# Attention and mixture of experts on one core: conditional weight copies for the first expert tiles, a shorter square root, W2's maxima on ScalarE, and a new order

## The chip, the core and the metric

The kernel runs on one core of one Trainium2 chip, as one program. Its time is device microseconds (us) of one execution. The engines of the core are TensorE (PE, with its weight loads as PEld), VectorE (DVE), ScalarE (ACT), GpSimd (POOL) and SyncE (SP, which here only issues DMA transfers).

## What is computed

An attention with pooled keys feeds a mixture of experts; every row goes to the one expert with the highest logit.

```python
# attention: B, N, C = 4, 12288, 128
kv_pool = kv.reshape(B, 96, 4, 8, 4, C).mean(axis=(2, 4))
k = v = kv_pool.reshape(B, 768, C) @ w_sr
s = (q @ k.transpose(0, 2, 1)) / sqrt(C)
a = exp(s - s.max(-1)); a /= a.sum(-1) + 1e-9
x = (a @ v).reshape(49152, C)
# experts: E, F = 8, 1024
xn = x / (norm(x) + 1e-6); en = emb / (norm(emb) + 1e-6)
logits = xn @ en.T / tau
expert = argmax(logits); gate = softmax(logits)[expert]
for e in range(E):
    out[expert == e] = gate * (relu(x[expert == e] @ w1[e]) @ w2[e])
```

## The kernel before

**Steps, groups and tiles.** The 49152 rows are 96 steps of 512 rows (24 per batch). A step loads its q (`q_load`), transposes it, multiplies it with k in four quarters (`s_mm`, 128 rows by 768 keys each), takes the maximum of each quarter (`s_max`, DVE), the exponential (`s_exp`, ACT), splits the result into a high and a low half (`p_hi` on ACT or DVE, `p_lo` on DVE or POOL), turns both by transposing DMAs (`p_t`) and multiplies them with v (`av`), then normalizes (`x_norm`, `x_mul`). In the first `kf` steps ("unscaled") s is computed in f32 from one copy of k instead of from f16 halves; the pairs of quarters marked in `em` ("unsplit") are transposed on PE (`p_turn`) and multiplied in f32, with no transposing DMA.

Four steps are a group: `group_ops` computes norms, logits, gates and the rank of every row within its expert and scatters the 2048 rows into `xs_rows`, a buffer sorted by expert (POOL, `g_scatter`). Per group, `select` then chooses the next 8 expert tiles (256 rows of one expert each) and writes for each its expert (`et`), its first row (`off_i`) and the row of its weights (`wi_i`); it runs on DVE for the first `sd` groups and on POOL for the rest, as a chain of small operations. The chain for the first 8 tiles (n = 0) starts when group 1 is ranked.

An expert tile loads its rows (`load`, L1551 and L1552) and its weights (`load_w`, L1541) into one of three weight buffers of 1026 KB, multiplies with W1 (`l1`), splits into `hh` (ACT, L1582) and `hl` (DVE, L1587), multiplies with W2 (`l2`), scales (`o_out`) and scatters into the output. For tiles marked A in `om` the gate is first multiplied with the scale that lies behind the weights (`o_gate`, L1622, DVE), and ACT writes the output; for the others DVE does it in one operation.

**Conditional copies.** The SP instruction of `load_w` copies only if `w < E * P`. `weight_rows` adds 4096 to the row when the tile has the same expert as the tile three before, whose weights are still in that buffer. It does so from tile 8 on; the first 8 tiles have no comparison and always copy.

**Weights.** `w_ops` loads W1 and W2 of each expert in the first 180 us, takes their maxima on DVE (`w_max`, L1187), makes a power of two from them (`pow2`), splits both into f16 halves and stores them to `w_prep`.

**Key and value pooling.** For batches 1 to 3, `kv_load` fetches each batch's keys in 8 pieces of 768 KB (L449), and DVE adds up each piece with four operations (`kv_adds`, L463).

**The order.** Each engine runs its instructions in the order in which they were written. That order comes from a planner (`Plan.run`): each piece of work has an engine, a duration, a key (its due time) and its dependencies, and the planner writes the ready piece with the lowest key. Transfers are modelled by `moved`, one running sum of the durations given as `dma`. The keys come from the numbers in `X`: `da` and `di` (length of a step), `kv` and `kvs` (how many steps ahead pieces of keys are loaded, and how far apart), `kv1` and `kvs1` (the same for batch 1), `lead` (how far ahead a tile's rows are loaded), and the strings of letters that choose an engine for each repetition of an operation. 16 steps (`ka`) run before the first expert tile; from there to step 96 each step is mixed with two expert tiles.

## Time and profile before

| | |
|---|---|
| runs of the kernel | 1978.6, 1984.32, 1983.66 us; median 1983.66 us |
| the profiled execution | 1983.56 us; its span from the first to the last instruction is 1981.9 us |
| TensorE's granted clock, mean | 0.992 of full speed |
| PE busy | 1921.1 us (97%) |
| PEld busy | 1687.6 us (85%) |
| DVE busy | 1695.6 us (86%) |
| ACT busy | 1531.0 us (77%) |
| POOL busy | 1254.1 us (63%) |
| DMA | 335.86 MB, mean 169 GB/s |

Busy times are unions of the instructions of an engine; shares are of the span. A matmul that runs while the granted clock is low counts as busy for longer. A mean duration times a count can be above the busy time, since neighbours overlap by some tens of ns.

### The profile page before, as it was taken

How to read it: one execution, taken by the hardware profiler on the slowest of the kernel's cores; microseconds unless marked ns; L12 is line 12 of the kernel's file. 1: busy time of each engine (PE TensorE's matmuls, PEld its weight loads, DVE VectorE, ACT ScalarE, POOL GpSimd, SP SyncE). 2: the span in 40 equal slices, each digit the busy share in tenths (PEclk: the TensorE clock that was granted, in tenths of full speed). 3: DMA queues.
4: the chain of work that ended last, by engine and by line, in shares of the span. 5: the costliest groups of instructions: out<-in, count | busy, mean ns of one | idle time of the engine just before them, and what ended most of it. 6: DMA issues, size and time to landing. Idle time of an engine off the chain costs nothing. (4 is left out here: it accounts for less than half of the span.)

```text
span 1981.9 us, 63458 instructions
## 1 busy us (share of the span) xinstructions
PE 1921.1 (97%) x23400; PEld 1687.6 (85%) x23400; DVE 1695.6 (86%) x3870; ACT 1531.0 (77%) x3343; POOL 1254.1 (63%) x1828
## 2 busy tenths in 40 slices
PE   6999889999999999999999989999999999999997
PEld 4777678888888888888888878888888888899997
DVE  7799979999899988989999979988988888886654
ACT  3876867888888878888888868888888888775443
POOL 1547566685676676675875756756756766666653
PEclk9999999999999999999999999999999999999999
DMA  8996999998899998888988998788878878762261
GB/s 278 225 245 177 216 225 197 182 184 154 170 182 171 186 207 172 165 164 163 173 177 171 175 210 172 165 149 164 175 155 166 154 159 149 141 135 75 67 132 51
DMA packets 880475, 335.86 MB, mean 169 GB/s; under 512 B 828050, under 2 KB 839451, under 8 KB 877856
## 3 DMA queue, kind: packets, MB, share of 16 engines
q1 hardware_dynamic: 853088, 276.99, 71.7%
q0 software_dynamic: 24704, 53.53, 9.9%
q8 instruction: 185, 3.03, 0.6%
q10 hardware_dynamic: 2368, 1.25, 0.2%
q14 instruction: 130, 1.06, 0.2%
HBM read 263.01 MB, written 64.50 MB: 165 GB/s over the span
## 5 line engine op out<-in xcount | busy, mean ns | idle before, releaser
L1575 PE MATMUL ph<-x,wbuf 128*128 128x256 f16 x4536 | 615.8, 273 | 18.5 <-DVE hl L1587 14.1
L1582 ACT ACTIVATE hh<-ph 128x512 f16<-128x512 f32 x756 | 451.4, 598 | 190.6 <-PE ph L1575 151.7
L205 POOL DMA_INDIRECT out_dram<-o,m x388 | 417.3, 1075 | 280.0 <-ACT o L1631 63.6
L1587 DVE SCALAR_TENSOR_TENSOR hl<-ph,hh 128x512 f16<-128x512 f32 x756 | 515.4, 683 | 91.0 <-ACT hh L1582 85.3
L205 POOL DMA_INDIRECT xs_rows<-rows,pi x384 | 438.4, 1142 | 200.7 <-issue 32.6
L1575 PEld LDWEIGHTS <-wbuf 128*128 128x128 f16 x4656 | 432.9, 98 | 81.2 <-issue 18.0
L1611 PE MATMUL po<-wbuf,hh 128*128 128x128 f16 x6048 | 461.5, 220 | 1.5 <-DVE hl L1587 1.3
L1611 PEld LDWEIGHTS <-hh 128*128 128x128 f16 x6208 | 405.1, 98 | 29.6 <-issue 2.9
L815 DVE TENSOR_REDUCE nm<-s 128x1 f32<-128x768 f32 x384 | 364.1, 949 | 45.4 <-PE s L806 33.0
L806 PE MATMUL s<-k,qT 128*128 128x512 f16 (+1 forms) x1920 | 365.5, 327 | 2.9 <-ACT qT L768 1.3
L844 ACT ACTIVATE p<-s,nm,qa 128x768 f32<-128x768 f32 x320 | 317.5, 992 | 33.1 <-DVE nm L834 26.9
L931 PE MATMUL xp<-v,pthi 128*128 128x136 f16 x4416 | 323.6, 223 | 2.1 <-DVE t_cnt L1311 0.8
L885 DVE TENSOR_TENSOR plo<-p,phi 128x768 f16<-128x768 f32 x320 | 307.1, 961 | 2.3 <-ACT phi L868 1.8
L1611 PE MATMUL po<-wbuf,hl 128*128 128x128 f16 x3024 | 292.8, 220 | 0.1
L931 PEld LDWEIGHTS <-pthi 128*128 128x128 f16 x4416 | 281.8, 97 | 7.7 <-issue 2.7
L806 PEld LDWEIGHTS <-qT 128*128 128x128 f16 x1920 | 179.9, 98 | 90.3 <-issue 2.5
L868 ACT CAST phi<-p 128x768 f16<-128x768 f32 x289 | 240.8, 837 | 10.9 <-DMA pthi<-phi 7.2
L1611 PEld LDWEIGHTS <-hl 128*128 128x128 f16 x3104 | 206.3, 98 | 1.0 <-DVE hl L1587 0.3
L931 PE MATMUL xp<-v,ptlo 128*128 128x136 f16 x2208 | 193.0, 223 | 2.7 <-DMA ptlo<-plo 2.7
L951 ACT ACTIVATE x<-xp,rn 128x135 f32<-128x135 f32 x304 | 97.0, 373 | 80.0 <-DVE rn L943 64.4
L931 PEld LDWEIGHTS <-ptlo 128*128 128x128 f16 x2208 | 147.5, 98 | 3.0 <-DMA ptlo<-plo 2.9
L965 POOL TENSOR_TENSOR rows<-x,rows 128x256 f16<-128x256 f32 x192 | 133.5, 701 | 18.5 <-ACT rows L961 14.6
(402 smaller groups left out, 2050.2 us busy)
## 6 DMA issues: line engine op xcount, KB each, us to landing
wbuf<-w_prep SPq DMA_DIRECT2D x194, 1026.0 KB
q<-in_q_dram SPq DMA_DIRECT2D x96, 256.0 KB
kvt<-in_kv_dram SPq DMA_DIRECT2D x24, 768.0 KB
wf<-in_moe_w_dram SPq DMA_DIRECT2D x16, 512.0 KB
out_dram<-o,m POOLq DMA_INDIRECT x388
kvt<-in_kv_dram SPq DMA_DIRECT2D x12, 512.0 KB
xs_rows<-rows,pi POOLq DMA_INDIRECT x384
w_prep<-wo SPq DMA_DIRECT2D x8, 514.0 KB
```

Source lines behind the costliest of these rows:

```text
L205: ins = nc.gpsimd.indirect_dma_start(out=dst[:, :], out_offset=bass.IndirectOffsetOnAxis(ap=idx, axis=0), in_=src, in_offset=None, bounds_ ...
L806: nc.tensor.matmul(t[:, lo:hi], qs[:, l, :], r[:, lo:hi], start=i == 0, stop=i == 2)
L815: V.tensor_reduce(out=nm, in_=ks[k]["s", j], axis=AX.X, op=ALU.max, negate=True)
L844: nc.scalar.activation(out=p, in_=ks[k].pop(("s", j)), func=AF.Exp, bias=ks[k].pop(("nm", j)), scale=1.0 if unscaled(k) else ks[k]["fac"],)
L868: nc.scalar.copy(out=hi, in_=p)
L885: eng.tensor_tensor(out=lo, in0=ks[k].pop(("p", j)), in1=hi, op=ALU.subtract)
L931: nc.tensor.matmul(ks[k]["xp", h][:, i, :e], l[:, c, :], r[:, c, :e], start=n == 0, stop=n == len(terms) - 1, skip_group_check=True,)
L965: nc.gpsimd.tensor_tensor(out=r[:, :, C : 2 * C], in0=ks[k]["x"][:, 2 * h : 2 * h + 2, 0:C], in1=r[:, :, 0:C], op=ALU.subtract)
L1575: nc.tensor.matmul(ph[:, kk * n : (kk + 1) * n], wt[:, o + f : o + f + P], r, start=i == 0, stop=i == 2)
L1582: nc.scalar.activation(out=hh, in_=ts[t]["ph", u], func=AF.Relu)
L1587: V.scalar_tensor_tensor(out=hl, in0=ts[t].pop(("ph", u)), scalar=0.0, in1=ts[t]["hh", u], op0=ALU.max, op1=ALU.subtract)
L1611: nc.tensor.matmul(ts[t]["po"][:, j * C : (j + 1) * C], h[:, kk * n + j * P : kk * n + (j + 1) * P], wt[:, f : f + P], start=u == 0 and i ...
```

## The change

1. `select` for the first 8 tiles also compares experts. `weight_rows` now builds the comparison for t0 = 0 too; `fresh` sets it to 0 for tiles 0 to 2, which have no tile three before.
2. `rsqrt` with three rounds of three operations becomes `root`: a guess of the square root, a reciprocal, a product, a sum, and again a reciprocal, a product and a weighted sum. The `norm` product behind it goes. That is 8 DVE operations instead of 12 for each of 24 groups, and once for the expert embeddings.
3. For every expert (`wq` is all A) the maximum of |W2| on DVE is replaced by a sum of squares on ACT (`w_sq`, 128x1024 with accumulation) and two small DVE operations (`w_norm`) that make a power of two from its root. Its junk output goes to the buffer `wo0`, which is so taken earlier.
4. The fill of the rows past all experts (`dummies`, 1152 KB, ACT's queue) moves from 30 us to step 88.
5. The planner's numbers are new: `kf` 14 instead of 16, 10 unsplit pairs instead of 8, `sd` 0 (the first `select` on POOL too), other letters for the engines, and other costs of transfers (`late` adds 8 us after a piece of keys, weights of the first three tiles cost 3.6).

```diff
 X = dict(
-    ka=16, da=8.163, di=15.077, db=14.187, dma=1.729, ahead=2.284, av=10.802, av0=0.255, lb=-2.941, l2=2.467,
-    qt=1.558, lead=18.764, x=-17.373, r=-0.479, s=-1.235, p=14.303, x0=5.348, r0=2.658, s0=1.425, p0=5.773, qt0=0.912,
+    ka=16, da=5.621, di=18.693, db=14.346, dma=1.729, ahead=2.284, av=10.385, av0=-0.933, lb=-2.362, l2=2.65,
+    qt=1.523, lead=26.836, x=-82.128, r=-0.415, s=-1.976, p=13.972, x0=2.656, r0=5.014, s0=1.344, p0=7.404, qt0=0.282,
...
-    h=13.626, kv=20.599, kvs=2.297, w0=-12.3, start=17.487, early=21.36, wd=13.046, xw=1.718, qd=23, qs=16.452,
+    h=19.587, kv=27.46, kvs=2.934, w0=-19.499, start=8.415, early=21.36, wd=11.49, xw=1.718, qd=24, qs=17.772,
...
-    kf=16, kc="AD", kk=4.522, su=-1.263, vk=-3.85, om="DDAAADAD", og=2.102,
+    kf=14, kc="DA", kk=0.062, su=1.242, vk=-1.844, om="DDDAADDD", og=1.947,
 )
...
-                        ready = self.moved + X["dma"]
+                        ready = self.moved + X["dma"] + op.late
...
-        def square():
-            V.tensor_tensor(out=h["z"], in0=y(), in1=y(), op=ALU.mult)
-        def times():
-            V.scalar_tensor_tensor(out=h["z"], in0=h["z"], scalar=-0.5, in1=x(), op0=ALU.mult, op1=ALU.mult)
-        def update():
-            V.scalar_tensor_tensor(out=y(), in0=h["z"], scalar=1.5, in1=y(), op0=ALU.add, op1=ALU.mult)
-        return [halve, guess] + [square, times, update] * 3
+        def under():
+            V.reciprocal(out=h["z"], in_=y())
+        def over():
+            V.tensor_tensor(out=h["z"], in0=h["z"], in1=x(), op=ALU.mult)
+        def twice():
+            V.tensor_tensor(out=y(), in0=y(), in1=h["z"], op=ALU.add)
+        def mean():
+            V.scalar_tensor_tensor(out=y(), in0=y(), scalar=0.25, in1=h["z"], op0=ALU.mult, op1=ALU.add)
+        return [halve, guess, under, over, twice, under, over, mean]
...
+    def w_sq(e):
+        w_out(e, 0)
+        nc.scalar.activation(out=ws[e]["wo", 0][:, 0:F], in_=ws[e]["w", 1], func=AF.Square, accum_out=ws[e]["m"][:, 1:2])
...
+        def fresh():
+            V.memset(h["same"][:, 0:WB], 0.0)
...
-        return [weights, same, skip, cast] if t0 >= WB else [weights, cast]
+        return [weights, same, *([] if t0 else [fresh]), skip, cast]
...
-    x_dummies = add("ACT", 0.1, 30.0, dummies, dma=3.1, hold=True)
+    x_dummies = add("ACT", 0.1, slot(NSTEP - 8, 0), dummies, dma=3.1, hold=True)
...
-            o = took("kvt", add("SP", 0.45, t0, lambda h=h: kv_load(b, h), *turn("kvt", 2), dma=2.6, hold=True))
+            o = took("kvt", add("SP", 0.45, t0, lambda h=h: kv_load(b, h), *turn("kvt", 2), dma=2.7, hold=True, late=8.0))
...
-                m.append(add("DVE", 1.14, v + 0.9 * d, lambda e=e, i=i: w_max(e, i), o, *deps))
...
+                if i and X["wq"][e] == "A":
+                    o = took("wo0", add("ACT", 1.2, v + 0.9 * d, lambda e=e: w_sq(e), o, *deps, *turn("wo0", 1)))
+                    m.append(add("DVE", 0.36, v + 0.9 * d, lambda e=e: w_norm(e), o))
```

What this moves is shown at three places. In the rows, a name ends in a number that grows in the order in which the planner wrote the program, so a piece of work with a higher number was written later; `hl_3_25893` is the low half of the fourth block of a tile's hidden units.

The first place is SP's queue at the second change of experts (tiles 96 to 98), where three copies of weights are made in a row and pieces of batch 3's keys are loaded. Before:

```order
L1541 DMA wbuf_2844<-w_prep 128x4104
L449 DMA kvt_6_25625<-in_kv_dram 96x4x512
L909 DMA_TRANSPOSE ptlo_1_25652<-plo_1_25493 128x12x128
L1547 TENSOR_LOAD off_i
L1547 ISA x2
L1551 ISA
L1551 DMA_TRANSPOSE x_25731<-xs_rows 128x2x256
```

And now:

```order
L1554 DMA wbuf_2927<-w_prep 128x4104
L909 DMA_TRANSPOSE pthi_1_25435<-phi_1_25139 128x12x128
L909 DMA_TRANSPOSE ptlo_1_25503<-plo_1_25196 128x12x128
L449 DMA kvt_7_25560<-in_kv_dram 96x4x512
L1552 TENSOR_LOAD wi_i
L1552 ISA x2
L1554 ISA
L1554 DMA wbuf_2928<-w_prep 128x4104
```

Before, a piece of keys followed the last of the three copies; now a piece (the last of the batch) lies between the second and the third.

The second place is DVE behind that load, where the piece is added up. Before:

```order
L1587 SCALAR_TENSOR_TENSOR hl_3_25679<-ph_3_25627,hh_3_25650 128x512
L815 TENSOR_REDUCE nm_2_25695<-s_156 128x1
L1419 TENSOR_REDUCE et<-t_lt_25593 128x8
L1587 SCALAR_TENSOR_TENSOR hl_0_25711<-ph_0_25672,hh_0_25697 128x512
L885 TENSOR_TENSOR plo_0_25648<-p_1_25567,phi_0_25520 128x768
L1587 SCALAR_TENSOR_TENSOR hl_1_25755<-ph_1_25703,hh_1_25735 128x512
L815 TENSOR_REDUCE nm_3_25781<-s_157 128x1
L1634 SCALAR_TENSOR_TENSOR o_25793<-po_25609,wbuf_2842,m_24554 128x256
L834 TENSOR_SCALAR nm_3_25781<-nm_3_25781,qa_24391 128x1
L1622 TENSOR_SCALAR m_25008<-m_25008,wbuf_2844 128x2
L463 TENSOR_TENSOR kvt_6_25625<-kvt_6_25625 96x1024
L1587 SCALAR_TENSOR_TENSOR hl_2_25834<-ph_2_25786,hh_2_25818 128x512
```

And now:

```order
L885 TENSOR_TENSOR plo_0_25837<-p_1_25811,phi_0_25816 128x768
L1600 SCALAR_TENSOR_TENSOR hl_3_25893<-ph_3_25857,hh_3_25880 128x512
L815 TENSOR_REDUCE nm_2_25917<-s_156 128x1
L1360 TENSOR_TENSOR t_same_25935<-et 128x8
L834 TENSOR_SCALAR nm_2_25917<-nm_2_25917,qa_24297 128x1
L463 TENSOR_TENSOR kvt_7_25560<-kvt_7_25560 96x1024
L1600 SCALAR_TENSOR_TENSOR hl_0_25957<-ph_0_25903,hh_0_25929 128x512
```

Three `hl` with numbers above the load's stood between the load and its first addition (25679, 25711, 25755), and a gate product that reads the weight buffer stood right before it; now six `hl` stand between them, and no gate product of a tile whose weights were just copied is there.

The third place is the choice of the first 8 tiles (n = 0). Before, on DVE:

```order
L1311 TENSOR_TENSOR t_cnt_2198<-base_124,basec 128x8
L815 TENSOR_REDUCE nm_2_2200<-s_157 128x1
L1301 SCALAR_TENSOR_TENSOR t_cnt_2198<-done,t_cnt_2198 128x8
L815 TENSOR_REDUCE nm_3_2230<-s_158 128x1
L1318 TENSOR_SCALAR t_nt_i_2255<-t_cnt_2198 128x8
```

And now, on POOL:

```order
L1321 TENSOR_TENSOR t_cnt_2065<-base_124,basec 128x8
L1314 TENSOR_SCALAR t_part_2071<-done 128x8
L1315 TENSOR_TENSOR t_cnt_2065<-t_part_2071,t_cnt_2065 128x8
L1328 TENSOR_SCALAR t_nt_i_2085<-t_cnt_2065 128x8
L1345 TENSOR_TENSOR t_ex_2132<-t_cum_2126,t_nt_2117 128x8
L205 DMA xs_rows<-rows_117,pi_2109 397312x144
```

The chain moved from DVE to POOL, where it alternates with the scatters of its group, and where a fused operation becomes two.

## Rows read from the trace of the kernel before

**Rows 1.** Windows: busy us (and instructions) of PE, PEld, DVE, ACT, POOL; PEclk; DMA.

```profile
10.00:220.00 210.00, 194.72 (x1374) 150.22 (x1375) 183.20 (x431) 150.03 (x309) 106.61 (x107) 0.96 0.90 229
220.00:320.00 100.00, 87.19 (x1018) 74.17 (x1016) 81.76 (x194) 72.89 (x164) 54.90 (x87) 0.98 1.01 219
1145.00:1195.00 50.00, 43.27 (x503) 36.33 (x501) 38.70 (x88) 35.58 (x80) 28.44 (x44) 0.93 0.99 195
1200.00:1850.00 650.00, 649.72 (x8377) 581.36 (x8376) 555.27 (x1283) 523.29 (x1163) 431.63 (x666) 1.00 0.74 149
```

**Rows 2.** Timeline of SP's queue: start us, us, instruction; copies of weights, first expert tiles.

```profile
225.55 0.37 SPq L1541 DMA_DIRECT2D wbuf<-w_prep  x1
...
295.39 0.34 SPq L1541 DMA_DIRECT2D wbuf<-w_prep  x1
...
309.73 0.10 SPq L1541 DMA_DIRECT2D wbuf<-w_prep  x1
```

**Rows 3.** Timelines of ACT and PE in 280 to 290 us; in brackets the idle time before.

```profile
284.76 0.63 ACT L706 ACTIVATE qjunk<-q 128x512 bf16<-128x512 f32 x1 [4.69 <-DMA q<-in_q_dram]
...
286.74 1.44 PE L1575 MATMUL ph<-x,wbuf 128*128 128x256 f16 x6 [4.04 <-DVE hl L1587]
```

**Rows 4.** Timelines of SP, DVE and PE in 1178 to 1190 us.

```profile
1178.14 0.61 SPq L449 DMA_DIRECT2D kvt<-in_kv_dram  x1
...
1183.78 0.23 DVE L1622 TENSOR_SCALAR m<-m,wbuf 128x2 f32<-128x2 f32 x1 [3.49 <-DMA wbuf<-w_prep]
1187.32 1.22 DVE L463 TENSOR_TENSOR kvt<-kvt 96x1024 f32<-96x1024 f32 x1 [3.31 <-DMA kvt<-in_kv_dram]
...
1189.19 1.44 PE L1575 MATMUL ph<-x,wbuf 128*128 128x256 f16 x6 [5.56 <-DVE hl L1587]
```

**Rows 5.** Lines of the whole trace: count, busy us and mean ns, idle us before.

```profile
L806 PE MATMUL s<-k,qT 128*128 128x512 f16 (+1 forms) x1920 | 365.5, 327 | 2.9 <-ACT qT L768 1.3 <-DVE k L587 0.9 <-ACT p L844 0.5
L931 PE MATMUL xp<-v,pthi 128*128 128x136 f16 x4416 | 323.6, 223 | 2.1 <-DVE t_cnt L1311 0.8 <-DVE w L660 0.7 <-DVE hl L1587 0.4
L931 PE MATMUL xp<-v,ptlo 128*128 128x136 f16 x2208 | 193.0, 223 | 2.7 <-DMA ptlo<-plo 2.7
L799 PE MATMUL s<-kf,qT 128*128 128x512 f32 (+1 forms) x256 | 95.7, 514 | 3.8 <-ACT p L844 2.3 <-DVE pw L903 1.1 <-DVE kf L576 0.4
L922 PE MATMUL xp<-v,pw 128*128 128x136 f32 x192 | 26.4, 299 | 3.2 <-DVE qT L748 3.2
L438 PE MATMUL s<-ident,p 128*128 128x128 f32 x96 | 12.7, 275 | 1.1 <-ACT p L844 1.0
```

**Rows 6.** The same view: operations that the change removes or moves.

```profile
L1187 DVE TENSOR_REDUCE wm<-wf 128x1 f32<-128x1024 f32 x16 | 19.2, 1203 | 0.0
L1062 DVE TENSOR_TENSOR y<-y,ss 128x16 f32<-128x16 f32 x24 | 4.5, 187 | 0.2
L1217 ACT ACTIVATE wo<-wf,w 128x1024 f16<-128x1024 f32 x3 | 3.4, 1149 | 1.3 <-DVE w L664 1.3
```

**Rows 7.** Timelines of DVE, POOL and PE: choice of tiles n = 0 and 1, first tile.

```profile
178.17 0.23 DVE L1311 TENSOR_TENSOR t_cnt<-base,basec 128x8 f32<-128x8 f32 x1
...
202.84 0.15 DVE L1360 CAST wi_i<-t_wi 128x8 int32<-128x8 f32 x1
...
231.44 2.12 PE L1575 MATMUL ph<-x,wbuf 128*128 128x256 f16 x18 [0.90 <-POOL rows L965]
...
237.06 0.20 POOL L1311 TENSOR_TENSOR t_cnt<-base,basec 128x8 f32<-128x8 f32 x1 [5.51 <-DVE base L1126]
...
281.51 0.20 POOL L1360 CAST wi_i<-t_wi 128x8 int32<-128x8 f32 x1
```

**Rows 8.** Timelines of DVE and POOL in 182 to 185 us; durations of one line.

```profile
182.26 2.10 DVE L1330 TENSOR_TENSOR_SCAN t_cum<-onesE,t_nt 128x8 f32<-128x8 f32 x1
...
182.21 2.12 POOL L1228 TENSOR_TENSOR wo<-wf,wo 128x1024 f16<-128x1024 f32 x1 [2.21 <-ACT wo L1219]
...
L885 POOL TENSOR_TENSOR plo<-p,phi x9: 1640/1648/1812, 39.0 to 89.2; 128x768 f16<-128x768 f32 x9
```

More of the change, by code (lines that the diff above doesn't have):

```diff
@@ L40 @@
 SELECT_TWO = ("left", "skip", "passed", "wrap", "begin", "lead_rows", "row")
[L41 removed]
+SELECT_DVE = ("fresh", "divide", "whole", "sums", "start", "after", "until", "expert", "first", "take", "same")
 X = dict(
[L46 to L55 removed]
@@ new lines @@
+    m=0.189, end=-3.858, ne=-10.151, ge=0.078, kd="DDD", gk=113.383, wq="AAAAAAAA", kv1=8.136, kvs1=0.474, tg=1.629,
+    tl=-0.73, qe="------------------------", gap=1.8, nb="--DDD-DADA--DDD--AD-AAD-AAD-----DAADA--DDDDD----",
+    sqm="AAAAAAAAAAASPAAAAPPAPPSA", qm="AAADDAADDAAADADAAAAADDAD", xh="DDPPAADAAAADAPADPDAPADAP", nl="-",
+    slack={'ACT PE': 0.065, 'ACT DVE': 0.127, 'ACT POOL': 0.461, 'ACT ACT': -0.082, 'DVE PE': 0.398, 'DVE ACT': 0.472, 'DVE POOL': 0.216, 'DVE DVE': -0.057, 'PE ACT': 0.103, 'PE DVE': -0.003, 'PE POOL': -0.1, 'PE SP': -0.11, 'POOL ACT': 0.46015762370487345, 'POOL DVE': 0.955, 'POOL PE': 0.1, 'POOL POOL': 0.07},
@@ L237, in attention_moe, with __init__ @@
     class Op:
-        def __init__(self, eng, dur, key, fn, deps, dma, take, free, hold, lands, port, stage):
+        def __init__(self, eng, dur, key, fn, deps, dma, take, free, hold, lands, port, stage, late):
             self.eng, self.dur, self.key, self.fn, self.dma = eng, dur, key, fn, dma
-            self.port = port
+            self.port, self.late = port, late
             self.take, self.free, self.lands, self.stage = take, free, lands, stage
@@ L260, in __init__, with add @@
             self.moved, self.stage = 0.0, 0
-        def add(self, eng, dur, key, fn, *deps, dma=None, take=None, free=None, hold=False, lands=False, port=False):
-            op = Op(eng, dur, key, fn, deps, dma, take, free, hold, lands, port, self.stage)
+        def add(self, eng, dur, key, fn, *deps, dma=None, take=None, free=None, hold=False, lands=False, port=False, late=0.0):
+            op = Op(eng, dur, key, fn, deps, dma, take, free, hold, lands, port, self.stage, late)
             self.ops.append(op)
@@ L1008, in x_sq_sum, with root @@
         )
-    def rsqrt(name, x, w, y):
+    def root(name, x, w, y):
         h = {}
@@ L1093, in onehot @@
             )
-        ops = rsqrt(f"n{g}", lambda: gr["ss"], GT, lambda: gr["y"])
-        return ops + [norm, guard, invert, logits, top, shift, hits, first, onehot]
+        ops = root(f"n{g}", lambda: gr["ss"], GT, lambda: gr["y"])
+        return ops + [guard, invert, logits, top, shift, hits, first, onehot]
     def g_exp(g):
@@ L1212, in w_hi @@
     def w_hi(e, i):
-        if i == 0:
+        if i == 0 and X["wq"][e] == "D":
             w_out(e, 0)
@@ L1289, in dummies @@
         )
+        for key in (*keys, "loads"):
+            tc.declare_no_dep(ins.ins, group=key, reason="rows past all experts")
+        tc.add_to_no_dep_group("loads", ins.ins)
     ts = [dict() for _ in range(NTILE)]
```

48 lines of the change are left out of this document (23 added, 25 removed).

## The prediction

> **What bounds the kernel now.** I read the windows first, one for each stage. From 1200 to 1850 us PE is busy for 649.72 of 650.00 us at full clock, while DVE, ACT and POOL all have time to spare [rows 1]. So in a steady stage no work taken from DVE, ACT or POOL can gain anything; only less PE work, or less PE idle time and less time at a low clock, can. The windows show where the idle time is: 15.3 us from 10 to 220 us (clock 0.96), 12.8 from 220 to 320 (0.98) and 6.7 from 1145 to 1195 (0.93). In the last two the DMA engines are busy for 1.01 and 0.99 of the time, against 0.74 in the steady stage [rows 1]. About 60 us are idle in all (span less PE's busy time); the rest lies mostly at the start and the end and is the same for both kernels.
>
> Then the timelines, for what each stop is. Between 220 and 320 us, 8 copies of weights go out, the first at 225.55 and the last at 295.39, each 0.35 us on SP's queue; the next at 309.73 takes 0.10 us, because its condition fails and nothing is copied [rows 2]. While these copies run, a load of q comes late: ACT waits 4.69 us for it with other work queued behind, PE then waits 4.04 for `hl`, and its first matmuls afterwards take 1.44 us at the lower clock [rows 3]. At 1183.78 DVE waits 3.49 us for a copy of weights, which the gate product L1622 reads, and then 3.31 for the piece of keys that was loaded at 1178.14; PE waits 5.56 for the `hl` behind both [rows 4]. So the stops are a waiting instruction at the head of an in-order queue, and what it waits for is a transfer in a full DMA stage.
>
> **The change, part by part.** The sum is made against the profiled execution, 1983.56 us; its span is 1981.9, so 1.7 lies around it, and the median of the runs is 0.1 above it.
>
> *A. Conditional copies, tiles 0 to 7.* From the reference's inputs I worked out which expert each row goes to: all 12288 rows of batch 0 go to expert 0, so the first change of experts comes at tile 48, the second at tile 96. Tiles 0 to 2 must copy; tiles 3 to 7 now skip. Five copies of 1026 KB are 5.25 MB; at the 219 GB/s of that window they are 24 us of a DMA that is full for 100 us [rows 1, 2]. It would then be as busy as in the steady stage. I take 5/8 of the 12.8 us idle, 8.0, and 1 us for matmuls that no longer run at the lower clock: **-9**. Bounds: 0 (the stops come from other loads) and all of it, -12.8 less a low-clock loss of about 1.6, so -14.4.
>
> *B. The second change of experts.* Two things change in the order. DVE has no gate product right behind a fresh copy (the letter of the third tile goes from A to D), so its wait of 3.49 has nothing to hang on. And six `hl` instead of three now lie between a piece's load and its first addition. Three of them, with what stood between, went with 9.2 us, so the piece gets some 14 us or more by six instead of the 9.2 from 1178.14 to 1187.32 [rows 4]. Of the 6.7 us idle and about 2.6 of low clock (0.07 of 50, less the idle share) I take -7 of 9.3, because a piece of keys now lies between the second and the third copy and so can delay that copy: **-7**, bounds 0 and -9.3.
>
> *C. PE's work.* `kf` goes from 16 to 14 steps: 8 quarters of s go from f32 to f16 halves. A quarter is 1.50 us in f32 (95.7/64) and 1.14 in f16 (365.5/320) [rows 5]: -2.9. Ten unsplit pairs instead of eight: four quarters pay (26.4 + 12.7)/16 = 2.44 instead of (323.6 + 193.0)/368 = 1.40 [rows 5]: +4.2. Together **+1.3**; these are counts, so the bounds are narrow, 0 and +2.
>
> *D. The first 220 us.* DVE is busy for 183.2 of 210 us there [rows 1]. It loses eight maxima of W2, 8 x 1.203 = 9.6 us [rows 6], and gets 16 operations of about 0.15 for them, 2.4; the choice for n = 0 (24.8 us from 178.17 to 202.84 with other work between) leaves for POOL [rows 7]. Other letters bring some of that back: by counting operations of both orders before the first expert tile, DVE has 4.7 us less. ACT gets 8 x 1.15 (by the row of another 128x1024 activation [rows 6]), POOL some 15. Part of the 15.3 us idle has its cause on DVE, but part is the start of the pooling, which waits for keys from DMA. I take **-4**. The bound below is -15, all of the idle time; the bound above is +10, the eight squares on ACT, which can be late in front of `p` in the same way as DVE was.
>
> *E. What I cost at nothing, and what hides it.* The root: four operations fewer by 0.187 [rows 6] in each of 24 groups, 18 us of DVE, hidden behind PE (DVE is idle for 95 of the 650 us in the steady stage [rows 1]). Without that cover it would be a gain. The letters: about 88 us of ACT go, and POOL gets 44 more subtractions `plo` of 1.648 [rows 8] and some 35 other operations, 83 us; POOL has 218 us free of the 650 [rows 1]. The cost if this cover is gone is the second rival's. The dummies (1152 KB) move from a stage where DMA is 0.90 busy to one of 0.74 [rows 1]; there they are 8 us of transfer in front of no one. The choice n = 0 on POOL: the same chain for n = 1 takes 44.7 us there (237.06 to 281.71) against DVE's 24.8, and from the last row index to the first matmul of a tile another 5.9 (225.55 to 231.44) [rows 2, 7], together 50.6. From the chain's start to that matmul 53.3 us pass now (178.17 to 231.44), and in the new order about 11 us more of PE's work stand between: 64 against 50.6, 13 us to spare. If it were late nonetheless, the first tile would wait at the head of PE's queue for the excess, one for one.
>
> **Sum:** -9 - 7 + 1.3 - 4 = -18.7, so 1964.9, **1965 us**.
>
> **The rivals.**
> 1. *The stops return elsewhere.* The new numbers load keys earlier (`kv` 27 steps ahead) and move every queue; PE's idle time was a matter of which load is late by some us. If A and B come back as waits of `s_exp` or `hl` on q, `pthi` or keys at other places, only C and part of D stay: **about 1983**, no change. For it: the waits before are of 3 to 5 us, the size by which the planner's one sum for all transfers can be wrong. Against it: 5.25 MB are really gone from the fullest stage. 0.15.
> 2. *POOL holds DVE off (slower).* At 182.21 POOL starts a subtraction of 2.12 us; DVE's sum over 128x8, begun at 182.26, lasts 2.10 and ends with it [rows 8], while a like operation takes 0.23 [rows 7], and the PE wait of 3.21 is for a copy that DVE had queued behind [rows 5]. The change has 53 instead of 9 such POOL subtractions. If each of the 44 held DVE for its whole length, beyond the operation's own, that is up to 44 x 1.648 = 72.5 us of DVE; it has 286 us idle over the span, so most would be hidden. It decides when more than a third reaches PE (25 us, enough to undo 18.7 and 0.3%); at 40%, 29 us, the time is **about 1994**. Against it: POOL works 431.63 of 650 us in the steady stage with other operations, and PE idles only 0.28 us there [rows 1]; but the nine subtractions of before all lie between 39.0 and 89.2 us [rows 8], so no row shows them in that stage. 0.15. The Trainium skill, "SBUF — State Buffer", section "SBUF: two separate sides", says that VectorE and GpSimd share a port pair which is locked for a whole instruction, and that a VectorE operation with two SBUF inputs is blocked by a GpSimd one that reads SBUF; the row above agrees with that, and by that rule alone, with nothing hidden, the kernel would become slower.
> 3. *The copies do not skip* (the comparison comes out false for tiles 3 to 7). Then A is 0 and the rest stays: -9.7, **1974**. 0.05: the same comparison works from tile 8 on [rows 2].
> 4. *More goes.* Less DMA in the first tiles and a later start of keys take nearly all idle time of the three windows, 15.3 + 12.8 + 6.7 = 34.8 with +1.3 for C and some cold clock: **about 1948**. 0.10.
>
> **How the numbers follow.** The forecast (A, B and D within their bounds, time from 1955 to 1975) has 0.55. A measurement of this kernel tells about 0.3%, 6 us, from no change. Faster by more: the forecast, rivals 3 and 4, 0.70; the same: rival 1, 0.15; slower: rival 2, 0.15. The range of 8 in 10 goes from 1950, which leaves out half of rival 4, to 1987, which takes in rival 1 and leaves out rival 2.
>
> **What the changed kernel's profile would show.** A is right if the copies of tiles 3 to 7 take 0.10 us on SP and the DMA's share between 220 and 320 us falls to near 0.75 with PE's idle time there under 6 us. B is right if no DVE instruction waits for a weight buffer around the second change of experts and the first addition of a piece does not wait for DMA. C is right if the f32 s row has 224 matmuls and the unsplit row 240. D is right if PE idles under 12 us up to the first expert tile. E is wrong if the first `ph` waits for `x` or weights; rival 2 shows itself as small DVE operations of 1.5 to 2 us beside POOL's `plo`, and PE waits for `hl` or `nm` in the steady stage. What would make the prediction wrong: PE idle time in 1200 to 1850 us, where none was, or the same idle sums in the three windows as before.

## The result, and the profile after

The changed kernel takes 2000.32 us (median of 6 runs, 1994.61 to 2001.62) against 1981.74 us for the kernel before on the same chip: ratio 1.0083, 95% interval 1.0069 to 1.0097. The medians differ by 18.6 us; by the ratio, which the text goes by from here on, it is some 16.5 us slower. 18.7 us faster was forecast. The profiled execution took 2001.24 us, its span is 1999.5.

The windows of the changed kernel, the four of [rows 1] and one more (busy us and instructions of PE, PEld, DVE, ACT, POOL; PEclk; DMA share; GB/s):

```profile
10.00:220.00 210.00, 190.26 (x1284) 143.14 (x1285) 175.72 (x415) 149.50 (x293) 115.73 (x130) 0.97 0.81 211
220.00:320.00 100.00, 90.53 (x1093) 76.93 (x1092) 97.07 (x220) 74.86 (x160) 69.48 (x100) 0.99 0.96 191
1145.00:1195.00 50.00, 48.26 (x619) 42.77 (x617) 44.73 (x101) 39.58 (x86) 35.84 (x54) 1.00 0.96 185
1195.00:1245.00 50.00, 43.32 (x499) 36.65 (x497) 38.11 (x91) 33.17 (x70) 23.64 (x32) 0.93 0.85 183
1200.00:1850.00 650.00, 639.26 (x8178) 568.71 (x8175) 558.54 (x1254) 492.51 (x1056) 439.25 (x655) 0.99 0.77 151
```

PE idles 9.5 us instead of 12.8 from 220 to 320 us, as wished. But it idles 19.7 instead of 15.3 us before that. The second change of experts comes some 20 us later here (its three copies of weights go out at 1172.27, 1186.49 and 1195.55 us, before at 1149.38, 1163.69 and 1177.76), so the window from 1145 to 1195 us holds other work than before; the longest stop of that stage now stands behind 1195 (6.7 us of idle time in that window, where the kernel before has none). The stretch from 1200 to 1850 us, with 0.28 us of idle time before, now has 10.7. Of that, 6.5 belong to the later stage; another stretch, from 320 to 1100 us, has no change of experts but the first, and shows the same: PE is busy for 766.80 us there in this kernel and for 776.46 in the kernel before.

The lines that answer to [rows 5] and to the last of [rows 8]:

```profile
L806 PE MATMUL s<-k,qT 128*128 128x512 f16 (+1 forms) x1968 | 375.0, 327 | 9.5 <-ACT p L844 7.7 <-DMA qT<-q 1.7
...
L931 PE MATMUL xp<-v,pthi 128*128 128x136 f16 (+1 forms) x4368 | 319.4, 223 | 12.3 <-DVE hl L1600 9.1 <-ACT p L844 1.4 <-DVE w L660 0.7
...
L931 PE MATMUL xp<-v,ptlo 128*128 128x136 f16 x2184 | 190.4, 222 | 0.0
...
L885 POOL TENSOR_TENSOR plo<-p,phi 128x768 f16<-128x768 f32 x53 | 89.5, 1688 | 22.9 <-ACT phi L868 15.4 <-DVE phi L872 6.9
...
L799 PE MATMUL s<-kf,qT 128*128 128x512 f32 x224 | 85.8, 521 | 7.0 <-DVE pw L903 3.3 <-ACT p L844 3.2 <-ACT pw L901 0.3
...
L922 PE MATMUL xp<-v,pw 128*128 128x136 f32 x240 | 29.7, 280 | 0.4 <-DVE pw L903 0.4
...
L438 PE MATMUL s<-ident,p 128*128 128x128 f32 x120 | 15.6, 274 | 2.1 <-ACT p L844 1.9
```

PE's own work is as it was. What is new stands behind the bars: `av` (L931) now waits 9.1 us for DVE's `hl`, `s` (L806) waits 7.7 us for ACT's `p` where it was 0.5 [rows 5], and POOL makes 53 subtractions.

Two places in time order, DVE and POOL (and what PE does then):

```profile
152.32 2.27 DVE L1016 TENSOR_SCALAR n1z<-ss 128x16 int32<-128x16 int32 x1
...
151.77 0.99 POOL L205 DMA_INDIRECT xs_rows<-rows,pi  x1 [0.17 <-issue]
152.77 0.17 POOL L970 IOTA rows<- 128x4 int32 x1
152.89 1.65 POOL L885 TENSOR_TENSOR plo<-p,phi 128x768 f16<-128x768 f32 x1
...
155.71 1.61 PE L799 MATMUL s<-kf,qT 128*128 128x512 f32 x3 [3.06 <-DVE pw L903]
...
337.83 2.30 DVE L727 TENSOR_SCALAR qa<-qa,bs 128x2 f32<-128x2 f32 x1
...
337.09 1.04 POOL L205 DMA_INDIRECT xs_rows<-rows,pi  x1 [0.59 <-DVE o L1647]
338.16 0.34 POOL L1443 TENSOR_TENSOR t_hit<-t_hit,t_lead 128x64 f32<-128x64 f32 x1
338.44 1.66 POOL L885 TENSOR_TENSOR plo<-p,phi 128x768 f16<-128x768 f32 x1
...
342.00 0.27 PE L438 MATMUL v_m<-ident,m 128*1 128x128 f32 x1 [1.99 <-DVE t_first L1446]
```

An operation on 128x2 elements lasts 2.30 us and ends at 340.13, POOL's subtraction at 340.10; the other ends at 154.59, its neighbour at 154.54. Then DVE still has its queue to work off, and PE waits 3.06 and 1.99 us for something at the end of it. To count this I took, for every DVE instruction, what it lasts beyond the median of its kind (over 0.15 us), and put it down to the POOL instruction that overlaps it most: 32 DVE instructions are held beside `plo`, by 49.4 us in all, against 3 and 2.9 us in the kernel before. Where two held instructions overlap, this count takes the same time twice; as time of DVE it is 47.5 us.

Do the holds reach PE, or is it POOL's own work that comes late? Followed back from every PE stop of 0.2 us or more in 320 to 1100 and 1226 to 1850 us (16.8 us in all), through waits and through the order of each engine, the stops of 14.1 us lead within 15 us to a DVE instruction that was held beside `plo` by over 0.7 us. One of them (1.45 us) has a wait for POOL's choice of tiles on the way as well; in all, DVE waits 14 us for POOL's results in this kernel and 14 in the kernel before.

Which kinds are held is seen in the durations of single lines (min/median/max in ns):

```profile
L1600 DVE SCALAR_TENSOR_TENSOR hl<-ph,hh x756: 620/681/693, 246.5 to 1988.3; 128x512 f16<-128x512 f32 x189
...
L815 DVE TENSOR_REDUCE nm<-s x384: 892/947/959, 32.4 to 1789.2; 128x1 f32<-128x768 f32 x192
...
L1030 DVE TENSOR_TENSOR n16z<-n16z,ss x2: 161/162/164, 1311.7 to 1312.8; 128x16 f32<-128x16 f32 x2
L1030 DVE TENSOR_TENSOR n17z<-n17z,ss x2: 176/1234/2291, 1384.7 to 1387.6; 128x16 f32<-128x16 f32 x2
```

`hl` and `nm`, which read what PE wrote, are never long, in 756 and 384 instructions. The root's small products, from SBUF to SBUF, take 0.16 to 0.18 us or, when held, 0.9 to 2.3.

### The profile page after: what moved, and what is told of

Its sections match the earlier page's. It is cut to its first block, busy times and chain, and to the rows that moved or that the text cites. A ratio compares the mean times of both kernels' runs of the same rounds, so it can differ in the third digit from the quotient of the medians.

```text
span 1999.5 us, 63261 instructions
## 1 busy us (share of the span) xinstructions
PE 1925.7 (96%) x23420; PEld 1686.6 (84%) x23420; DVE 1727.9 (86%) x3843; ACT 1476.3 (74%) x3097; POOL 1334.0 (67%) x1901
## 3 DMA queue, kind: packets, MB, share of 16 engines
q10 hardware_dynamic: 2368, 1.25, 0.2%
## 5 line engine op out<-in xcount | busy, mean ns | idle before, releaser
L205 POOL DMA_INDIRECT xs_rows<-rows,pi x384 | 432.3, 1126 | 179.3 <-issue 37.6
L1588 PEld LDWEIGHTS <-wbuf 128*128 128x128 f16 x4656 | 425.8, 98 | 47.1 <-DMA wbuf<-w_prep 3.9
L806 PE MATMUL s<-k,qT 128*128 128x512 f16 (+1 forms) x1968 | 375.0, 327 | 9.5 <-ACT p L844 7.7
L844 ACT ACTIVATE p<-s,nm,qa 128x768 f32<-128x768 f32 x328 | 324.7, 990 | 73.2 <-DVE nm L834 65.2
L931 PE MATMUL xp<-v,pthi 128*128 128x136 f16 (+1 forms) x4368 | 319.4, 223 | 12.3 <-DVE hl L1600 9.1
L931 PEld LDWEIGHTS <-pthi 128*128 128x128 f16 x4368 | 279.8, 97 | 20.6 <-issue 15.3
L885 DVE TENSOR_TENSOR plo<-p,phi 128x768 f16<-128x768 f32 x287 | 278.0, 971 | 9.0 <-ACT phi L868 5.2
L806 PEld LDWEIGHTS <-qT 128*128 128x128 f16 x1968 | 190.9, 98 | 103.7 <-issue 10.5
L868 ACT CAST phi<-p 128x768 f16<-128x768 f32 x297 | 246.1, 832 | 8.2 <-DMA pthi<-phi 3.4
L931 PE MATMUL xp<-v,ptlo 128*128 128x136 f16 x2184 | 190.4, 222 | 0.0
L931 PEld LDWEIGHTS <-ptlo 128*128 128x128 f16 x2184 | 145.5, 98 | 0.0
L982 ACT ACTIVATE junk<-x 128x128 f32<-128x128 f32 x376 | 113.2, 306 | 14.4 <-DVE x L953 14.1
```

The lines of the kernel that those rows point to most:

```text
L205: ins = nc.gpsimd.indirect_dma_start(out=dst[:, :], out_offset=bass.IndirectOffsetOnAxis(ap=idx, axis=0), in_=src, in_offset=None, bounds_ ...
L806: nc.tensor.matmul(t[:, lo:hi], qs[:, l, :], r[:, lo:hi], start=i == 0, stop=i == 2)
L844: nc.scalar.activation(out=p, in_=ks[k].pop(("s", j)), func=AF.Exp, bias=ks[k].pop(("nm", j)), scale=1.0 if unscaled(k) else ks[k]["fac"],)
L868: nc.scalar.copy(out=hi, in_=p)
L885: eng.tensor_tensor(out=lo, in0=ks[k].pop(("p", j)), in1=hi, op=ALU.subtract)
L931: nc.tensor.matmul(ks[k]["xp", h][:, i, :e], l[:, c, :], r[:, c, :e], start=n == 0, stop=n == len(terms) - 1, skip_group_check=True,)
```

## The experiments

The first eight runs were on two chips on which the kernel before takes 2048.15 and 2046.78 us, the last eight, like the result, on chips where it takes 1982 to 1984; each ratio is to the kernel before on the same chip. The changed kernel was not run again beside the last eight: where they are set against it, its 1.0083 is that of the result. Two variants that keep POOL's subtractions, `a_uncond` and `a_wmax`, stood at 1.0137 and 1.0113 on the chip of `a_plo_memset`, 0.0173 and 0.0149 above it.

**1. Who subtracts (kernel before 2048.15).** `a_plo_dve`, from the changed kernel:

```diff
-        eng = V if p_mode(k, j)[1] == "D" else nc.gpsimd
+        eng = V
```

> The changed kernel with all 53 subtractions plo that POOL makes given to DVE at the same place of the order; the orders of PE, ACT and SP stay the same. Theory H (a POOL subtraction holds DVE off, and what is queued behind reaches PE late): the 49 us by which 32 DVE instructions beside a POOL plo were too long go, DVE gets about 53 x 0.97 = 51 us of its own instead, so its busy time stays near 1728 us; of the changed kernel's PE idle time about 20 us follow such a hold within 9 us, and half or more of it goes: 10 to 18 us faster than the changed kernel's 2000.3, 1982 to 1990, ratio to the kernel before 1.000 to 1.005. Rival L (DVE is late because the new letters give it 56 x, 46 o and 67 nm more): no gain, 2000 or more, ratio 1.008 or above.

Measured 0.9955 (0.9933 to 0.9977). The changed kernel itself, `a_again` (no edit), gave on the other chip of this kind:

> The changed kernel itself, unedited, beside the kernel before on the chip of these runs, for comparison with its variants. All theories: slower than before, ratio 1.008 as measured first (1.004 to 1.012), with some 50 us of DVE instructions held by POOL's plo.

Measured 0.9999 (0.9979 to 1.0020): on these chips it is as fast as the kernel before, so the expectation failed there (see the last section), although 30 DVE instructions are held, by 45.4 us. Against it `a_plo_dve` gains 0.44%, 9 us, though DVE then makes 53 more subtractions: just under theory H's 10 to 18 us, and against rival L.

`b_plo_pool`, the reverse, from the kernel before:

```diff
-        eng = V if p_mode(k, j)[1] == "D" else nc.gpsimd
+        i = NQ * k + j
+        pm, rest = "acbdbcdbcacbccbaadccabb", "acaabaaa"
+        m = pm[i] if i < len(pm) else rest[i % len(rest)]
+        eng = V if p_mode(k, j)[1] == "D" and m in "ab" else nc.gpsimd
```

> The kernel before with 40 of DVE's subtractions plo given to POOL, the same quarters as in the changed kernel, at the same place of the order; the orders of PE, ACT and SP stay the same. Theory H: some 24 of the 40 hold a DVE instruction for 1 to 2 us; PE idle time appears in the stretch from 1200 to 1850 us, where the kernel before has 0.28 us; 6 to 15 us slower, 1988 to 1997, ratio 1.003 to 1.008, although DVE has 38 us less of its own to do. Rival L: DVE has 38 us less to do, so no change or up to 5 us faster, ratio 0.997 to 1.001.

Measured 1.0083 (1.0063 to 1.0102): 17 us slower with less work on DVE. By the count above, 29 DVE instructions are held by 34.6 us. In the stretch that was named, 1200 to 1850 us, PE has idle time in every kernel on this chip and is no less busy here than in `b_cond` below (630.07 against 627.65 us; same chip, the same order, 9 subtractions on POOL), so the expectation failed as to the place. The loss shows in the windows from 520 to 1100 us of this kernel and of `b_cond`:

```profile
520.00:1100.00 580.00, 553.96 (x6909) 483.31 (x6907) 496.51 (x1116) 460.99 (x1017) 394.94 (x564) 0.99 0.85 165
```

```profile
520.00:1100.00 580.00, 568.71 (x7145) 498.20 (x7143) 511.70 (x1183) 474.47 (x1050) 381.64 (x558) 1.00 0.87 170
```

PE loses 14.8 us there. Not all of it need be the holds: with 40 more subtractions in front of it, POOL also chooses the tiles later, and DVE waits for that, 33 us in all against 17 in `b_cond`. The largest of these waits, in this kernel and in `b_cond` (us in total, times, longest):

```profile
DVE t_first L1436 <- POOL t_hit L1433: 15.6, 11, 3.9
```

```profile
DVE t_first L1437 <- POOL t_hit L1434: 7.3, 10, 2.4
```

How the 17 us divide between the two this run does not show; the changed kernel has no such growth (14 us, as before). `a_x_act` tests rival L:

```diff
-        if in_turn("xn", k, 2 * k + h) == "ACT":
+        if ("AA" if k < KA else "AAAD")[(2 * k + h) % (2 if k < KA else 4)] == "A":
```

> The changed kernel with x (x_mul) back on ACT where the letters of the kernel before have it; 56 operations leave DVE (24 us) for ACT (112 by 0.37, 41 us), POOL's subtractions stay. Theory H: the holds stay, PE idle time falls a little at most: 1995 to 2001, ratio 1.006 to 1.010. Rival L: DVE's load is what is late, so 8 to 18 us go: 1982 to 1992, ratio 1.000 to 1.005.

Measured 0.9995 (0.9973 to 1.0016), the changed kernel's own ratio: 24 us less on DVE gain nothing. That speaks against rival L but does not settle it: ACT is busy for 27 us more, the holds fell with the same edit from 45.4 to 34.0 us without a gain, and on these chips the changed kernel has no loss that could go.

**2. The parts of the code.** `b_cond`, the conditional copies alone in the kernel before (2048.15):

```diff
         def cast():
+            if not t0:
+                same()
+                V.memset(h["same"][:, 0:WB], 0.0)
+                skip()
             eng.tensor_copy(out=wi_i[:, t0:t1], in_=h["wi"])
```

> The kernel before with the conditional copies of the first 8 tiles alone, the three operations issued inside the step that made the cast, so that the order stays the same. The forecast's term A: five copies are skipped, the DMA's share between 220 and 320 us falls from 1.01 to about 0.75, PE idle there from 12.8 to under 5 us: 9 us faster, ratio 0.995 (0.993 to 0.998). Rival (the stops in that window are DVE's and ACT's, not the copies'): PE idle there stays above 9 us, ratio 0.998 to 1.002.

Measured 0.9945 (0.9919 to 0.9971), 11 us. Its windows:

```profile
220.00:320.00 100.00, 95.21 (x1156) 82.06 (x1155) 91.01 (x217) 76.90 (x174) 59.28 (x97) 1.00 0.92 183
```

PE idles 4.8 instead of 12.8 us [rows 1]. The DMA's share stays at 0.92, not 0.75: what followed moved up. `b_cond_root` adds the root (2046.78): the functions' bodies are those of `root`, in its order, and `guard` and the old `norm` are empty, so that the planner's steps stay:

```diff
-        return [halve, guess] + [square, times, update] * 3
+        return [halve, guess, square, times, update, square, times, norm, guard, guard, guard]
```

> The kernel before with the conditional copies and the shorter square root, in place: the order of PE, ACT and SP stays, DVE has four operations fewer per group (18 us in all). Forecast's E: the root's DVE time is hidden, so ratio as with the copies alone, 0.993 to 0.996. Rival: on a DVE that is busy for 85% of the span the root shortens chains that PE waits for: 0.988 to 0.992; or its reciprocals make it slower: 0.997 or above.

Measured 0.9944 (0.9922 to 0.9966), as without: the root's 18 us are hidden. Then both are planned anew: `a_oldx` is the changed kernel with the numbers of the kernel before, `b_newx` the kernel before with the new numbers.

```diff
-    ka=16, da=5.621, di=18.693, db=14.346, dma=1.729, ahead=2.284, av=10.385, av0=-0.933, lb=-2.362, l2=2.65,
+    ka=16, da=8.163, di=15.077, db=14.187, dma=1.729, ahead=2.284, av=10.802, av0=0.255, lb=-2.941, l2=2.467,
...
+    kf=16, kc="AD", kk=4.522, su=-1.263, vk=-3.85, om="DDAAADAD", og=2.102, wq="AAAAAAAA",
```

```diff
-    ka=16, da=8.163, di=15.077, db=14.187, dma=1.729, ahead=2.284, av=10.802, av0=0.255, lb=-2.941, l2=2.467,
+    ka=16, da=5.621, di=18.693, db=14.346, dma=1.729, ahead=2.284, av=10.385, av0=-0.933, lb=-2.362, l2=2.65,
...
```

> The changed kernel's code with the planner's numbers and letters of the kernel before (W2's squares on ACT stay): conditional copies, root and squares are there, POOL makes 9 plo again, the order is planned from the old numbers. Theory H (the new letters' POOL subtractions are what costs, the parts in the code are good): ratio 0.990 to 0.997, faster than before by the conditional copies' 0.5% and a little more. Rival P (one of the code's parts costs: squares on ACT in front of p, or the root): ratio 1.000 or above.

> The code of the kernel before with the new numbers and letters: no conditional copies for the first 8 tiles, the old reciprocal root, W2's maxima on DVE, but 53 plo on POOL and the new order. Theory H: slower than the changed kernel by the copies and the DVE work that stays, ratio 1.010 to 1.020. Rival P: faster than the changed kernel, ratio 1.000 to 1.006.

Measured 0.9996 (0.9975 to 1.0018) and 1.0163 (1.0141 to 1.0184). The second fits theory H: without the new code the new numbers lose 1.6%. The first misses theory H's 0.990 to 0.997 and comes out at rival P's end: on this chip the same code takes as long with the old numbers, where 3 DVE instructions are held beside `plo` by 4.4 us, as with the new, where it is 45.4. The 0.55% that the same copies gain in place were not had. The two do not share an order, so this does not separate the theories; but from 10 to 240 us PE waits 17.3 us for ACT's `p` in `a_oldx` and 3.3 in `b_cond_root`. The largest of these waits, first in `a_oldx`:

```profile
PE s L799 <- ACT p L844: 10.6, 8, 3.1
```

```profile
PE s L799 <- ACT p L844: 2.3, 2, 2.0
```

What of that is the order's and what the squares' on ACT stays open.

**3. The hold without DVE's price (kernel before 1983.81).** `a_plo_memset`, from the changed kernel:

```diff
-        eng = V if p_mode(k, j)[1] == "D" else nc.gpsimd
+        if p_mode(k, j)[1] == "P":
+            ks[k].pop(("p", j))
+            nc.gpsimd.memset(lo, 0.0)
+            return
+        eng = V
```

> The changed kernel, in which POOL fills the 53 low halves that it subtracted with zeros instead (the low half of these quarters is left out of the product): POOL still writes them at the same place of its order, but reads nothing, and DVE gets no more work. Theory H: DVE's holds beside plo go (34 to 49 us in the traces of the changed kernel and its variants) at no cost on DVE; the kernel before lost 17 us by 35 us of such holds, so 15 to 25 us less than the changed kernel itself: ratio 0.988 to 0.993 on a chip where that one stands at 1.000. Rival L or S (DVE's load, or the order itself, is what is late): 0 to 5 us, ratio 0.997 to 1.000.

Measured 0.9964 (0.9949 to 0.9979): 0.0119 below the changed kernel's 1.0083, 23.6 us (by the two intervals some 4 us either way), as theory H said, and faster than the kernel before. The two quiet stretches in its windows:

```profile
320.00:1100.00 780.00, 776.86 (x9870) 688.47 (x9868) 711.07 (x1613) 625.70 (x1327) 541.28 (x805) 1.00 0.89 174
1200.00:1850.00 650.00, 648.87 (x8391) 581.77 (x8389) 552.43 (x1275) 493.47 (x1049) 440.93 (x673) 1.00 0.73 146
```

POOL's row in its lines, and the durations of the root operation that was held above:

```profile
L886 POOL MEMSET plo<- 128x768 f16 x53 | 40.0, 757 | 10.4 <-DMA ptlo<-plo 10.3
```

```profile
L1034 DVE TENSOR_TENSOR n17z<-n17z,ss x2: 175/175/175, 1357.3 to 1358.0; 128x16 f32<-128x16 f32 x2
```

A DVE instruction that is still held, and POOL beside it, from its timelines:

```profile
581.87 1.54 DVE L717 TENSOR_SCALAR qa<-qa 128x2 int32<-128x2 int32 x1
...
581.63 1.00 POOL L205 DMA_INDIRECT out_dram<-o,m  x1 [0.87 <-DVE rn L946]
582.61 0.77 POOL L886 MEMSET plo<- 128x768 f16 x1
```

PE is as busy as in the kernel before (776.46 and 649.72), with the changed kernel's letters for all else. By the count above 16 DVE instructions are still held beside the filling, by 12.9 us; as time of DVE, without what overlaps, 8.5 us. So 39.0 of 47.5 us went, and if the gain of 23.6 is all theirs, three fifths had reached PE. The edit also gives POOL 49.5 us back (89.5 to 40.0); that this is what helped is unlikely by the stops followed back above, but no run separates it.

`a_uncond` undoes the conditional copies in the changed kernel:

```diff
         def skip():
+            if not t0:
+                return
             both(
```

> The changed kernel with the first 8 copies of weights unconditional again, the order unchanged. Term A: the five copies cost what they cost in the kernel before, 8 to 12 us, ratio 1.004 to 1.006 where the changed kernel stands at 1.000. Rival: under the new order (keys loaded earlier, other waits in that window) nothing, 0.999 to 1.002.

Measured 1.0137 (1.0108 to 1.0165), 0.54% or 10.7 us above the changed kernel; PE idles 13.5 us from 220 to 320 us. Term A again. `a_wmax` undoes W2's squares:

```diff
     def w_sq(e):
         w_out(e, 0)
-        nc.scalar.activation(out=ws[e]["wo", 0][:, 0:F], in_=ws[e]["w", 1], func=AF.Square, accum_out=ws[e]["m"][:, 1:2])
     def w_norm(e):
-        m = ws[e]["m"][:, 1:2].bitcast(I32)
...
+        w_max(e, 1)
```

> The changed kernel with W2's maxima on DVE again, in the place of the two small operations, and no squares on ACT; the order of the other work unchanged. Forecast's term D: DVE gets 8 x 1.2 us in the first 220 us, 2 to 6 us slower than the changed kernel, ratio 1.001 to 1.003. Rival P (the squares on ACT stand in front of p, which PE waits for from 110 to 220 us): 2 to 8 us faster, ratio 0.996 to 0.999.

Measured 1.0113 (1.0082 to 1.0144): 6 us above the changed kernel, though the intervals overlap. It speaks for the forecast and against rival P: from 10 to 240 us PE still waits 11.9 us for ACT's `p` without the squares, 11.2 in the changed kernel with them. `b_best` is `b_cond_root` with an edit at the second change of experts:

```diff
     def o_gate(t):
+        if t in (50, 98):
+            return
...
-        if gated(t):
+        if gated(t) and t not in (50, 98):
...
+                if (b, h) == (3, 6) and (out is first or later):
+                    later.append(fn)
...
         ts[t]["hl", u] = hl
+        if later:
+            past.append(t)
+            if len(past) == 3:
+                for fn in later:
+                    fn()
+                later.clear()
```

> The kernel before with the conditional copies and the shorter root in place, and at the second change of experts what the forecast's term B speaks of: the third tile's gate product goes (DVE writes its output), and the four additions of the piece of keys that was late are issued three hl later. Term B: of the 5.5 us that PE stops there 4 or more go, ratio 0.990 to 0.993 against 0.9944 without. Rival: the stop moves to the next wait for the same transfers, ratio 0.994 to 0.996.

Measured 0.9924 (0.9900 to 0.9948), 1968.2 us: better than both kernels. Against 0.9944, which is from the other kind of chip, the intervals overlap; the trace has seven stops of 0.34 to 1.03 us from 1170 to 1202 us, 4.3 in all, in place of one of 5.6 [rows 4]; the granted clock from 1145 to 1195 us is 1.00 where it was 0.93.

**4. What was still open (kernel before 1981.83).** The stop behind 1195 us in the changed kernel, its timelines of SP, ACT and PE:

```profile
1195.55 0.36 SPq L1554 DMA_DIRECT2D wbuf<-w_prep  x1
...
1198.65 5.38 SPq L909 DMA_TRANSPOSE pthi<-phi  x1
...
1214.96 1.09 SPq L698 DMA_DIRECT2D q<-in_q_dram  x2
...
1218.83 0.63 ACT L706 ACTIVATE qjunk<-q 128x512 bf16<-128x512 f32 x1 [4.70 <-DMA q<-in_q_dram]
...
1219.46 0.47 ACT L560 ACTIVATE pT<-pp 128x384 f32<-128x384 f32 x1
...
1193.07 0.83 PE L1588 MATMUL ph<-x,wbuf 128*128 128x256 f16 x6 [1.74 <-DMA wbuf<-w_prep]
...
1204.28 0.83 PE L1588 MATMUL ph<-x,wbuf 128*128 128x256 f16 x6 [1.64 <-DVE nm L834]
...
1219.99 1.65 PE L565 MATMUL kp<-pT,wsr 128*128 128x384 f32 x2 [4.83 <-ACT pT L560]
```

The transpose lasts 5.38 us on SP's queue against 1.42 some 13 us later; the load of q goes out behind it, ACT stands in front of it with the pooled keys `pT` queued behind, and PE waits. That is the stop of [rows 3] at another place. With the two smaller stops in front of it the stage costs PE 8.2 us; before it was 6.4 (0.61, 0.18 and the 5.56 of [rows 4]). `a_ms_q` is `a_plo_memset` with that operation moved:

```diff
+        if k == 68:
+            ks[k]["late"] = square
+            return
+        if k == 69:
+            ks[68].pop("late")()
+        square()
```

> The changed kernel with POOL's 53 low halves filled with zeros (left out, as in a_plo_memset) and one more edit: the sum of squares of step 68's q, for which ACT waits in front of the pooled keys of batch 3, is issued behind them, in the place of step 69's. Theory Q (term B's gain was not had because the stop moved to this late load of q): the PE stop of 4.7 us in front of the product of the pooled keys falls under 2.5 us and 2 to 4 us go, ratio 0.994 to 0.996 against 0.9964 for a_plo_memset. Rival: the pooled keys are late themselves, the stop stays, 0.996 to 0.998.

Measured 0.9955 (0.9938 to 0.9972). The stop in front of `kp` is gone, but two others stand there:

```profile
1175.28 1.46 PE L1601 MATMUL ph<-x,wbuf 128*128 128x256 f16 x6 [3.54 <-DMA wbuf<-w_prep]
...
1204.55 0.27 PE L438 MATMUL v_m<-ident,m 128*1 128x128 f32 x1 [2.84 <-DVE m L681]
```

The stop went as theory Q says and nothing measurable is won: the wait for the same copy of weights was 1.25 us in `a_plo_memset`, and `v_m` had none there. `a_ms_w` is `a_plo_memset` with no weight work on ACT for expert 7:

```diff
+        if e == 7:
+            nc.gpsimd.memset(hi, 0.0)
+            return
         if w_eng(e, i) == " AD":
```

> The changed kernel with POOL's 53 low halves filled with zeros and, for expert 7 alone, no scaling and no high half of the weights on ACT (POOL fills them with zeros; the weights of that expert are left out). Theory W (between 205 and 240 us PE waits for p because ACT has the last expert's weights in front of it): the stops of 1.2, 2.6, 0.8 and 2.6 us there fall to 4 us or less in all and 3 to 6 us go, ratio 0.993 to 0.995. Rival: ACT is full there with q, phi and p themselves; 0 to 2 us, 0.995 to 0.997.

Measured 0.9962 (0.9948 to 0.9976), no change. The stops of 1.22, 2.64, 0.80 and 2.56 us for `p` are now 0.18, 1.80, 1.15 and 2.56, so a part of them was the weights'; but a new stop of 2.82 us stands between them, for `ptlo`, which had none. Theory W's gain was not had. `a_fix` keeps the result, with the edits of `a_plo_dve` and `a_ms_q`:

> The changed kernel with two edits that keep its result: the 53 plo on DVE, and step 68's sum of squares behind the pooled keys. Theory H with the DVE time that it costs, and theory Q: 12 to 20 us of the 24 to 28 us that stand between the changed kernel and a_ms_q: ratio 0.998 to 1.002 where the changed kernel stands at 1.008 (0.992 to 0.995 where it stands at 1.000). Rival: DVE's 51 us more give all of it back, ratio as the changed kernel's.

Measured 0.9984 (0.9971 to 0.9997): 1.0% or 20 us less than the changed kernel. `b_best_wo`, in the order of the kernel before:

```diff
-            nc.gpsimd.tensor_tensor(out=lo, in0=ws[e]["w", i], in1=hi, op=ALU.subtract)
+            (V if (e, i) == (7, 1) else nc.gpsimd).tensor_tensor(out=lo, in0=ws[e]["w", i], in1=hi, op=ALU.subtract)
```

> b_best with one of POOL's 13 subtractions of weights (the last, which runs at 182 us beside DVE's t_cum) on DVE instead. Theory H: t_cum takes 0.2 instead of 2.1 us, the PE stop of 3.2 us behind it goes, DVE has 1.3 us more: 1 to 3 us, ratio 0.991 to 0.992 against 0.9924. Rival: DVE's own 1.3 us delay the same copy, no change, 0.992 to 0.993.

Measured 0.9920 (0.9900 to 0.9939), 1964.28 us, the fastest of all; against `b_best` no difference that can be measured. DVE and PE in `b_best`, then in `b_best_wo`:

```profile
181.04 2.09 DVE L1348 TENSOR_TENSOR_SCAN t_cum<-onesE,t_nt 128x8 f32<-128x8 f32 x1
...
183.78 2.62 PE L934 MATMUL xp<-v,pw 128*128 128x136 f32 x15 [3.21 <-DVE qT L760]
```

```profile
181.16 0.15 DVE L1348 TENSOR_TENSOR_SCAN t_cum<-onesE,t_nt 128x8 f32<-128x8 f32 x1
...
182.31 1.22 DVE L1246 TENSOR_TENSOR wo<-wf,wo 128x1024 f16<-128x1024 f32 x1
...
181.97 3.05 PE L934 MATMUL xp<-v,pw 128*128 128x136 f32 x24 [1.27 <-DVE qT L760]
```

With POOL's subtraction away the same instruction takes 0.15 us, and the stop falls by 1.9 us.

## Why the prediction was wrong

**The step that failed most is E, "the letters".** It priced 44 more subtractions on POOL at nothing because POOL has 218 us free, and left DVE's hold to the second rival with a chance of 0.15. That rival's mechanism is what happened. The holds came to 47.5 us of DVE's time, where it had reckoned with up to 72.5; of them more reached PE than its 40%, about three fifths (23.6 of 39.0 us). Its time, 1994 us, was 6 us low. On the chips of `a_again` the changed kernel has the same holds and is no slower than the kernel before, so this price is shown for one kind of chip. The sentence that misled was "it has 286 us idle over the span, so most would be hidden". DVE's idle time is an average; a hold of 1.5 to 2 us falls in front of the next `hl`, and DVE's queue, 86% full, gives PE the delay on before it has caught up. The one row of the trace of before that showed such a hold [rows 8] also showed a PE wait behind it, and `b_best_wo` confirms that pair. That row should have weighed more than the share.

By itself this step would have left the kernel about 5 us slower (23.6 less 18.7). The forecast missed by 35.2 us; the other 11.6 are B and D, up to 15.6 us worse than forecast, less the 4.0 by which A and C came out better.

**A was right**: -9 forecast; -11 in the old order (`b_cond`), 10.7 in the new (`a_uncond`). The copies of tiles 3 to 7 do skip (0.08 to 0.10 us on SP), so rival 3 is out; the last that copies and the first that does not:

```profile
249.04 0.34 SPq L1554 DMA_DIRECT2D wbuf<-w_prep  x1
...
259.88 0.10 SPq L1554 DMA_DIRECT2D wbuf<-w_prep  x1
```

Only the picture of DMA falling to the steady share was wrong.

**B failed**, -7 forecast. The order did what was said on DVE: around the second change no gate product and no first addition of a piece waits for a transfer any more. But PE's stops there are 8.2 us in place of 6.4: it now waits itself for a copy of weights (1.74) and, at 1220 us, 4.83 for pooled keys that stand behind a late load of q. The step took it that the stop goes with DVE's waits; the DMA stayed as full (0.96), and another load was late instead. It is rival 1's mechanism, in one stage only, and `a_ms_q`, in which the next stop came up again, fits it.

**C was right** in kind, a small term, if below its bounds of 0 and +2: the six rows of PE's lines changed by +9.5, -4.2, -2.6, -9.9, +3.3 and +2.9, together -1.0 us, where +1.3 was forecast.

**D failed** in sign: -4 forecast, PE idles 4.5 us more from 10 to 220 us, 1.5 more without the subtractions (193.18 us busy in `a_plo_memset` against 194.72). The W2 part looks right (`a_wmax`, 6 us, not resolved); what gives it back are waits of PE for ACT's `p`, 11.2 us from 10 to 240 us where the kernel before has 3.3. They are the way that the upper bound named, but not for its reason: they stay without the squares (`a_wmax`) and for the most part without the last expert's weights on ACT (`a_ms_w`). Their cause the runs did not settle.

**E's other parts held**: the root is hidden (`b_cond_root`), and the first `ph` (at 244.99 us) waits for nothing, so the choice n = 0 was in time. Together: A 10.7 and C 1.0 gained, the holds 23.6 lost; to come to the measured +16.5, B and D must have lost up to 4.6 us in place of gaining 11 (less if the holds that were left in `a_plo_memset` cost anything).

## What to carry to other kernels

Work that goes to POOL is not free for DVE: look in the trace for small SBUF operations of DVE that take ten times their usual length beside a POOL instruction, and price each further POOL operation by these rows and by who waits behind them, not by the idle share of either engine. A stop that came from a late transfer in a full DMA stage moved here when the order changed (the second change of experts, `a_ms_q`); it went where bytes went, with the conditional copies.
